# Attention and a low-rank mixer on one core: off-diagonal keys kept in place, later q and k turned by VectorE blocks and TensorE products, and another order of the work

## The chip, the cores and the metric

The kernel runs on one core of one Trainium2 chip. The core has TensorE (matrix products, with PE in the profile; its weight loads are PEld), VectorE (DVE), ScalarE (ACT), GpSimd (POOL) and SyncE (SP), and 16 DMA engines that move data between HBM and on-chip memory (SBUF). Products land in PSUM, which has eight banks. Each engine runs its own list of instructions in the order in which the program issued them, and waits on semaphores for the others. The metric is device time in microseconds (us), the median of three runs.

## The reference

Four sequences of 768 tokens with 8 heads of 64 go through attention with a sliding window and a few global keys, and the result through a mixer and a two-layer network:

```
scores = q @ k.T / 8 - slope[h] * dist        # dist: distance back, 96 for a global key outside the window
keep   = (key < 8) or (0 <= query - key < 96)
x      = softmax(scores where kept) @ v       # heads side by side: (4, 768, 512)
h      = (x.T @ U @ V).T                      # U: 768 x 32, V: 32 x 768
u      = x + h
out    = u + relu(u @ w1) @ w2                # w1: 512 x 2048, w2: 2048 x 512
```

Inputs and output are float32; the kernel computes in float16 with float32 sums.

## The kernel before, in words

The work is cut into 16 *pairs* (batch `b`, two heads), `p = 4b + hp`, each done by `attention(p)`, and four batches of `mlp(b)`. Tokens come in six blocks of 128.

**Loads (`add_load`, lines 439 to 496).** q, k and v of a pair are fetched from float32 HBM into float16 staging tiles by DMAs that GpSimd issues (`lk`, `lq`, `lv`; lines 453, 457, 461). Pairs 0 to 6 fetch rows of several tokens in one DMA; pairs 7 to 15 fetch q and k in two DMAs each, with 64 numbers of one token (256 B in HBM, 128 B in SBUF) as the piece. The weights come in eight DMAs (`w1_`, `w2_`; L503, L512), also from GpSimd.

**Turning (`EK`, `EQ`).** Scores need q and k with the 64 features on the partitions. Pairs 0 to 6 are turned by TensorE (`tr`, L600: twelve transposes of 128x64 each for q and for k, on half of the array's columns) and copied out of PSUM by ScalarE or VectorE. Pairs 7 to 15 are turned by DMA transposes issued from SyncE (L624).

**Off-diagonal keys.** A block of 128 queries looks at its own block of keys and at 96 keys of the block before together with 32 slots that hold the global keys. For k the 32 global columns are appended to every block (`KO`, one copy of 128x5x32), and the product reads columns 32 to 160. For v the 96 rows must move by 32 partitions (`vo`): GpSimd does it in three copies for pairs 0 and 1, and a DMA from SyncE (L651) for the others; a fourth copy on GpSimd brings the global rows (L368).

**Attention.** For batch 0 a bias product (`SB`, L689: identity times a table per head) comes ahead of the scores (`S`, L708); for later batches the exponential (`EX`, L735, ScalarE) is multiplied by a mask (`MK`, VectorE). `PV` (L804, L805) multiplies by v with a column of ones for the sums; `RC` and `NM` divide; `XC` casts x to float16; `UP` (L778, L788) turns x by products with the identity and multiplies it by U; `TE` copies x.T U out, `HM` (L911) multiplies by V, and `E` copies u, turned, to `uT`. For pairs 12 to 15 x is turned by a DMA transpose instead (`XD`, L880), and VectorE adds it in `E`.

**Network.** `M1a`/`M1b` (L967) are 512 products of 384 columns, `RL` (L984) the relu on ScalarE. The second layer multiplies 2x2 blocks with seven products (`P1` to `P7`, L1047) instead of eight, with sums on VectorE before (`PA`, `PB`) and after (`DA` to `DH`, L1060); `O` stores rows from SyncE.

**Order.** Nothing is issued as it is written. `add` collects tasks with an engine, an assumed duration, what they need and which buffers they take. `Planner.run` plays them through, and where several tasks of an engine are ready it takes the one with the lowest number in the table `PRIO`; the resulting start times sort the program. In the first part, where the plan leaves TensorE without work, products of zeros (`idle`, L1118) are put in.

Of the kernel before, what the change touches and what calls it, by code (L numbers as in the profile page):

```python
# [16 lines left out]
PE, ACT, DVE, POOL, SP = "PE", "ACT", "DVE", "POOL", "SP"  # L17


PRIO = {  # L20
    "DA0.1": 9974.7, "DA1.1": 2084.0, "DA1.2": 1446.2, "DA2.1": 7573.6, "DA2.2": 168.5, "DB0.0": 381.3,
    "DB0.1": 824.4, "DB0.2": 1435.8, "DB1.0": 648.9, "DB1.1": 9380.8, "DB1.2": -715.0, "DB2.0": 1750.3,
    "DB2.1": 7394.5, "DB2.2": 921.0, "DB3.0": 4247.8, "DB3.1": 1752.8, "DC0.0": 1445.9, "DC0.1": 241.1,
    "DC0.2": 3950.9, "DC1.2": -1125.0, "DC3.0": 4597.3, "DD0.0": -369.8, "DD0.1": 1451.6, "DD0.2": 7547.4,
    "DD1.0": 5644.0, "DD1.2": 1790.9, "DD2.2": 1857.9, "DD3.0": 9079.6, "DE0.0": 4526.5, "DE0.1": 4818.3,
    "DE0.2": 1899.6, "DE1.0": 1079.9, "DE1.1": 1235.7, "DE1.2": 9688.2, "DE2.0": 9329.5, "DE2.1": 7182.2,
    "DE3.1": 408.9, "DF0.0": -587.1, "DF0.1": 906.3, "DF0.2": 1308.3, "DF1.0": 1987.4, "DF1.1": 4335.1,
    "DF1.2": 9220.2, "DF2.1": 1119.2, "DG0.0": 1566.3, "DG0.1": 1561.2, "DG0.2": 4753.1, "DG1.1": 1049.2,
    "DG2.0": 1258.8, "DG3.0": 8393.9, "DH0.1": -943.2, "DH0.2": 7144.0, "DH1.0": 4329.3, "DH1.2": 1416.7,
    "DH2.0": 1090.1, "DH2.2": 9290.0, "E01": 680.8, "E012": 6952.3, "E015": 6662.8, "E02": 1709.4,  # L30
    "E03": 7455.6, "E115": 6744.6, "EK1": 1092.1, "EK11": 1175.1, "EK2": -4286.2, "EK3": 1889.8,
    "EQ0": 5977.3, "EQ1": 1795.7, "EQ2": 3871.2, "EQ3": 1123.3, "EQ4": 2337.6, "EQ5": -70.1,
    "EX0.0": 136.1, "EX0.1": 619.4, "EX0.2": 1542.8, "EX1.0": -44.8, "EX1.2": 651.6, "EX10.0": -3388.7,
    "EX10.1": -4484.6, "EX11.0": 671.9, "EX12.0": 259.7, "EX12.1": 848.5, "EX13.1": 2805.7, "EX14.0": -4053.9,
    "EX15.0": 325.5, "EX15.1": 1245.1, "EX2.2": 459.5, "EX3.2": -4609.0, "EX4.0": 2040.9, "EX4.1": 708.4,
    "EX5.1": -3545.6, "EX5.2": 2671.0, "EX6.0": 277.4, "EX7.1": 1490.6, "EX8.0": 484.1, "EX8.1": 473.6,
    "EX9.0": -4173.8, "EX9.1": 528.5, "HM1": 7237.6, "HM10": 1056.5, "HM11": 2789.4, "HM12": 193.4,
    "HM13": 4578.0, "HM14": 2924.3, "HM4": 1390.4, "HM6": 6847.2, "HM7": 7112.0, "HM8": 875.8,
    "KO1": 4413.7, "KO10": 4820.4, "KO13": 1045.3, "KO4": 1558.1, "KO6": 7458.7, "KO8": 810.0,
    "KO9": 5696.5, "MK10.1": -64.6, "MK10.2": 8941.2, "MK11.0": 1790.4, "MK11.1": 6926.2, "MK11.2": 4176.4,  # L40
    "MK12.1": 9457.0, "MK12.2": 9396.4, "MK14.0": 1575.4, "MK15.0": 2089.4, "MK5.0": 1157.0, "MK5.1": 4456.1,
    "MK5.2": 4026.8, "MK6.1": 1969.0, "MK6.2": 8473.4, "MK7.0": 1965.2, "MK7.2": 8877.9, "MK8.0": 4742.7,
    "MK8.2": 7363.9, "NH3.0": 1052.5, "NH3.1": 4293.2, "NH3.2": -718.0, "NM0": 3502.3, "NM10": -3.6,
    "NM12": 745.7, "NM13": 4324.7, "NM2": 956.8, "NM3": 8933.0, "NM4": 6531.1, "NM6": 9302.7,
    "NM8": 8671.5, "NM9": 5709.1, "P10.0": 8038.9, "P10.1": 3749.7, "P10.2": 1100.2, "P11.0": 7486.8,
    "P11.1": 779.5, "P11.2": 890.3, "P12.0": 258.9, "P12.1": 1917.5, "P12.2": -195.3, "P13.0": 1231.1,
    "P13.1": 5474.6, "P13.2": 1092.0, "P20.0": 6169.2, "P20.1": 6444.0, "P20.2": 1493.3, "P21.0": 81.1,
    "P21.1": 196.4, "P21.2": 6738.9, "P22.0": 7741.1, "P22.1": 7201.7, "P22.2": 4091.2, "P23.0": -41.9,
    "P23.1": 1721.9, "P23.2": 7210.2, "P30.0": 7173.3, "P30.1": 6570.0, "P30.2": 1800.3, "P31.0": 7984.8,
    "P31.1": 4608.1, "P31.2": 1074.6, "P32.0": 284.8, "P32.1": 7089.9, "P32.2": 738.2, "P33.0": 8514.1,  # L50
    "P33.2": 9035.8, "P40.0": 8007.7, "P40.1": 3973.5, "P40.2": 6133.8, "P41.0": 3854.4, "P41.1": 7361.7,
    "P41.2": 6492.4, "P42.1": 7111.9, "P42.2": 1850.0, "P43.0": 5388.4, "P43.1": -217.2, "P43.2": 8297.9,
    "P50.0": 7151.2, "P50.1": 7171.5, "P50.2": 1808.9, "P51.0": 6511.1, "P51.1": 3837.9, "P51.2": 806.0,
    "P52.0": 2789.2, "P52.1": 7444.2, "P52.2": 988.2, "P53.0": 3222.2, "P53.1": 8488.0, "P53.2": 5964.3,
    "P60.0": 1544.3, "P60.1": 7428.3, "P60.2": 6759.4, "P61.0": 3319.6, "P61.1": 3970.3, "P61.2": 5190.3,
    "P62.0": 6224.9, "P62.1": 7152.4, "P62.2": 804.9, "P63.0": 4221.3, "P63.1": 480.6, "P63.2": 802.1,
    "P70.0": 6565.8, "P70.1": 8670.9, "P70.2": 4740.0, "P71.0": 6930.4, "P71.1": 3484.2, "P71.2": 2866.8,
    "P72.0": 5944.4, "P72.1": 7444.2, "P72.2": 7101.8, "P73.0": 5747.6, "P73.1": 6207.0, "P73.2": 4226.5,
    "PA0.1": 3875.7, "PA1.1": 4773.6, "PA2.3": 4018.7, "PB0.0": 4368.4, "PB0.1": 3979.1, "PB1.0": 4691.2,
    "PB1.1": 4947.3, "PB1.2": 581.7, "PB1.3": 5664.9, "PB2.1": 9613.8, "PB2.2": 6977.8, "PB2.3": 1205.4,  # L60
    "PV1": 953.8, "PV10": 6764.8, "PV11": 1576.6, "PV12": 7016.6, "PV13": 4620.5, "PV14": 4609.9,
    "PV2": 4453.8, "PV3.1": 7591.7, "PV3.2": 6559.2, "PV4": 3559.8, "PV5": 5520.0, "PV6": 6732.0,
    "PV8": 8381.2, "PV9": 6620.1, "RC1": 1068.7, "RC10": -348.8, "RC3.0": 85.5, "RC3.1": 1705.7,
    "RC3.2": 1515.9, "RC4": 1577.1, "RC5": 572.7, "RC6": 9411.2, "RC9": 4947.8, "RS0.0": 623.7,
    "RS0.1": 7972.9, "RS0.2": -1247.9, "RS1.0": 667.2, "RS1.1": 4419.1, "RS1.2": 657.7, "RS2.0": 6902.5,
    "RS2.1": 3723.0, "RS2.2": 7418.7, "RS3.0": 200.0, "RS3.1": -174.3, "RS3.2": 8.1, "S0.0": 1224.9,
    "S0.1": 1257.7, "S0.2": 597.8, "S1.1": 6958.1, "S1.2": 408.5, "S10.2": 925.1, "S11.0": 2116.4,
    "S11.2": 2864.1, "S12.0": 7724.4, "S12.2": 1228.1, "S13.0": 2772.6, "S13.2": 6865.5, "S14.0": 1199.9,
    "S14.2": 2407.7, "S15.0": 1398.4, "S15.2": 4794.4, "S2.0": 7510.6, "S2.2": 4999.8, "S3.0": 1728.1,
    "S3.2": 3575.4, "S4.0": 7303.6, "S4.2": 7813.1, "S5.0": 7633.1, "S5.2": 6453.5, "S6.0": 1492.8,  # L70
    "S6.2": 2826.3, "S7.0": 2695.5, "S7.2": 5594.9, "S8.0": 6717.1, "S8.2": 6990.7, "S9.0": 3459.0,
    "S9.2": 6262.8, "SB0.0": 1291.1, "SB0.1": 514.3, "SB0.2": 7692.8, "SB1.0": 430.4, "SB1.1": 599.9,
    "SB1.2": 4615.8, "SB2.0": 7063.3, "SB2.1": 4782.3, "SB2.2": 7308.6, "SB3.0": 531.8, "SB3.1": 6967.6,
    "SB3.2": 6911.1, "TD0": 7030.0, "TE0": 3966.3, "TE1": 675.6, "TE10": 4461.6, "TE11": 280.5,
    "TE12": 4818.6, "TE13": 4022.1, "TE14": 1818.3, "TE2": 4322.3, "TE3": 1059.7, "TE5": 4885.8,
    "TE6": -68.9, "TE7": 251.6, "TE8": 9276.7, "TE9": 4286.1, "TK4": 7905.3, "TK5": 5413.1,
    "TK6": 4414.1, "TQ1": 2668.8, "TQ2": 7693.4, "TQ3": 6828.5, "TQ5": 1864.3, "TQ6": 4764.5,
    "TWa0": 9550.6, "UP0": 7074.6, "UP1": 7827.2, "UP10": 2854.9, "UP11": 953.4, "UP12": 6809.4,
    "UP13": 7067.4, "UP14": 1956.0, "UP15": 791.9, "UP2": 6544.2, "UP3.0": 7443.0, "UP4": 3868.9,
    "UP5": -1290.3, "UP6": 7978.5, "UP7": 8833.1, "UP8": 5191.3, "UP9": 2150.7, "VO1.0": 7116.1,  # L80
    "VO1.2": -3290.1, "VO10": 1203.0, "XC0": 7540.7, "XC1": 1666.3, "XC10": 7434.6, "XC15": 2000.5,
    "XC2": -2725.2, "XC4": 6510.6, "XC5": 7203.3, "XC6": 7832.2, "XC7": -638.1, "back": 5810.4,
    "bias0": 1175.4, "bias1": 986.6, "bias2": 2210.6, "bias3": 7209.7, "bias4": 8335.5, "bias5": 1191.5,
    "bias6": 6089.3, "bias7": 7006.4, "lk1": -135.8, "lk11": 6090.1, "lk15": 7280.7, "lk2": 972.8,
    "lk3": 6441.1, "lk4": 7540.3, "lk5": 7421.1, "lk6": 7505.4, "lq1": 927.0, "lq13": 4852.5,
    "lq2": 6424.7, "lq3": 6999.5, "lq4": -3610.8, "lq5": 7812.9, "lv0": 5693.9, "lv1": 7056.6,
    "lv15": 7968.8, "lv2": -2525.5, "lv3": 8233.4, "lv4": 6565.3, "lv5": 9127.7, "lv8": 7499.0,
    "mask0": 2297.1, "mask1": 589.7, "mask2": 775.8, "mask3": 1722.4, "mask4": 1692.7, "mask5": 2036.9,
# [176 lines left out]
def kernel(  # L265
# [13 lines left out]
    nc = tc.nc  # L279
# [888 lines left out]
```

## Time and profile before

| what | value |
|---|---|
| median of 3 runs | 234.32 us (233.78 to 234.71) |
| profiled execution, first to last instruction (its span) | 231.3 us |
| median less span | 3.0 us |
| granted TensorE clock | 1.000 |
| TensorE busy | 223.4 us, 97% |
| VectorE busy | 153.1 us, 66% |
| ScalarE busy | 118.7 us, 51% |
| GpSimd busy | 90.2 us, 39% |

The span is the profiled execution's own time on the engines; no separate total of that execution is given, so the 3.0 us between it and the median of the other runs is taken as what lies around the span. TensorE is the engine to follow: it has almost no idle time after the first 30 us. A matmul's busy time in the profile includes its way through the array, so products that follow each other overlap in it; the rate is read from the distance between starts. A "first part" below means the time until the first `M1a`, at 35.1 us.

### The profile page before, as it was taken

The page shows a single profiled execution, that of the slowest core. Times are in us where ns is not written, and L with a number is a line of the kernel's source. Part 1 is how long each engine was busy: PE and PEld are TensorE (multiplying, and loading weights), DVE is VectorE, ACT ScalarE, POOL GpSimd, SP SyncE. Part 2 cuts the span into 40 slices and gives each one's busy share as a digit, 9 for nine tenths or more (in the row PEclk, how much of TensorE's full clock was granted, in tenths as well). Part 3 has the DMA queues.
Part 4 walks back from the last instruction along what each step waited for, and adds up shares of the span by engine and source line. Part 5 has one row for each costly group of instructions (what it writes and reads, how often), then busy time and mean ns, then how long its engine had stood idle before and what let it go on. Part 6 is the DMA issues. An engine that isn't in the chain of part 4 may idle for free.

```text
span 231.3 us, 5732 instructions
## 1 busy us (share of the span) xinstructions
PE 223.4 (97%) x2402; PEld 158.3 (68%) x2402; DVE 153.1 (66%) x321; ACT 118.7 (51%) x161; POOL 90.2 (39%) x116
## 2 busy tenths in 40 slices
PE   7889999999999999999999999999999999999993
PEld 2556675565788885656678885666689875658882
DVE  6548772499987975375867785395888840626762
ACT  3576978878632446766652228868610025662000
POOL 9789968349929960264800911030100000000000
PEclk9999999999999999999999999999999999999999
DMA  7999999999999999992961995221020630000025
GB/s 169 162 163 150 156 189 211 207 188 166 167 157 160 175 166 235 219 123 22 130 56 41 162 162 173 56 41 30 15 22 17 157 136 4 0 0 3 0 84 191
DMA packets 89642, 26.96 MB, mean 117 GB/s; under 512 B 77040, under 2 KB 86640, under 8 KB 89616
## 3 DMA queue, kind: packets, MB, share of 16 engines
q0 software_dynamic: 63616, 13.24, 69.3%
q1 hardware_dynamic: 26000, 13.35, 27.3%
q8 instruction: 19, 0.31, 0.5%
q14 instruction: 7, 0.06, 0.1%
HBM read 27.46 MB, written 6.29 MB: 146 GB/s over the span
## 4 chain that ended last, share of the span: by engine, by line
PE 84%; POOL 7%; DMA 6%; issue 1%; ACT 0%; DVE 0%; POOLq 0%
PE ps L967 37%; PE ps L1047 33%; PE ps L708 4%; DMA vt<-in_v_dram 3%; DMA stgk<-in_k_dram 3%; PE ps L805 2%; PE ps L788 2%; POOL vo L368 2%; PE ps L804 2%; PE ps L1035 1%; POOL stgk L453 1%; POOL vt L461 1%; PE ps L778 1%; PE ps L911 1%; POOL stgq L453 1%
## 5 line engine op out<-in xcount | busy, mean ns | idle before, releaser
L967 PE MATMUL ps<-uT,w 128*128 128x384 f16 x512 | 88.1, 326 | 0.3 <-ACT uT L364 0.3
L967 PEld LDWEIGHTS <-w 128*128 128x128 f16 x512 | 48.1, 98 | 32.2 <-issue 1.0
L984 ACT ACTIVATE htr<-ps 128x768 f16<-128x768 f32 x64 | 51.9, 811 | 32.4 <-PE ps L967 32.2
L735 ACT ACTIVATE ep<-ps 128x1024 f16<-128x1024 f32 (+1 forms) x48 | 44.1, 952 | 16.0 <-PE ps L708 15.9
L1047 PEld LDWEIGHTS <-htr 128*128 128x128 f16 x384 | 36.1, 98 | 6.5 <-issue 2.0
L1047 PEld LDWEIGHTS <-sA 128*128 128x128 f16 x288 | 27.5, 98 | 3.8 <-issue 0.5
L461 POOL DMA_DIRECT2D vt<-in_v_dram x16 | 16.5, 1031 | 34.4 <-PE ps L805 27.9
L748 DVE TENSOR_TENSOR ep<-ep,mask 128x1024 f16<-128x1024 f16 x24 | 16.6, 691 | 16.4 <-ACT ep L735 16.4
L1060 DVE TENSOR_TENSOR x_sb<-ps,x_sb 128x256 f32<-128x256 f32 x48 | 19.9, 421 | 9.9 <-PE ps L1047 9.4
L1047 PE MATMUL ps<-w,htr 128*128 128x256 f16 x192 | 24.5, 273 | 0.0
L1047 PE MATMUL ps<-tB,htr 128*128 128x256 f16 x192 | 24.4, 273 | 0.0
L1047 PE MATMUL ps<-w,sA 128*128 128x256 f16 x192 | 24.4, 273 | 0.0
L368 POOL COPY vo<-vt 32x650 f16<-32x650 f16 x22 | 18.1, 823 | 9.5 <-DMA vt<-in_v_dram 8.9
L1001 DVE TENSOR_TENSOR sA<-htr 128x768 f16<-128x768 f16 x16 | 9.5, 594 | 18.3 <-ACT htr L984 18.1
L364 ACT ACTIVATE u<-ps 128x256 f32<-128x256 f32 x12 | 4.6, 384 | 29.7 <-PE ps L1047 29.7
L869 POOL CAST x<-x_sb 128x768 f16<-128x768 f32 x12 | 10.8, 906 | 22.7 <-DVE x_sb L843 12.8
L457 POOL DMA_DIRECT2D stgk<-in_k_dram x18 | 14.8, 834 | 3.8 <-PE ps L967 3.8
L708 PEld LDWEIGHTS <-kT 64*128 64x128 f16 x352 | 10.1, 94 | 8.9 <-issue 8.1
L457 POOL DMA_DIRECT2D stgq<-in_q_dram x18 | 14.9, 838 | 3.1 <-DMA w<-in_moe_w_ch_dram 3.1
L708 PE MATMUL ps<-qT,kT 64*128 64x128 f16 x352 | 15.6, 218 | 0.0
L843 DVE TENSOR_TENSOR x_sb<-ps,rcp 128x768 f32<-128x768 f32 x16 | 15.2, 956 | 0.4
L1060 DVE TENSOR_TENSOR u<-ps,u 128x256 f32<-128x256 f32 x24 | 10.0, 419 | 6.7 <-PE ps L1047 4.9
(78 smaller groups left out, 272.2 us busy)
## 6 DMA issues: line engine op xcount, KB each, us to landing
out_dram<-x_sb SPq DMA_DIRECT2D x23, 256.0 KB, 2.6
w<-in_moe_w_ch_dram POOLq DMA_DIRECT2D x8, 512.0 KB, 9.2
vt<-in_v_dram POOLq DMA_DIRECT2D x16, 192.0 KB, 7.1
stgk<-in_k_dram POOLq DMA_DIRECT2D x18, 96.0 KB, 6.8
stgq<-in_q_dram POOLq DMA_DIRECT2D x18, 96.0 KB, 6.2
vo<-vt SPq DMA_DIRECT2D x14, 121.9 KB, 4.9
stgk<-in_k_dram POOLq DMA_DIRECT2D x6, 192.0 KB, 6.7
stgq<-in_q_dram POOLq DMA_DIRECT2D x6, 192.0 KB, 6.6
```

The costliest lines, as they stand in the source:

```text
L368: nc.gpsimd.tensor_copy(dst, src)
L457: nc.gpsimd.dma_start(o[:, :, hi], src[b, h0 + hi].rearrange("(n p) d -> p n d", p=P))
L461: nc.gpsimd.dma_start(vt[gv.slot][:, :, :, 0:D], v[b, h0:h0 + 2].rearrange("h (n p) d -> p h n d", p=P),)
L708: nc.tensor.matmul(t[:, hi, j * P:(j + 1) * P], lhs, qt[r, i * P:(i + 1) * P], start=not biased, stop=True, skip_group_check=biased,)
L735: nc.scalar.activation(ep[gep.slot][:, :, lo:512], ps[:, gsc.slot:gsc.slot + 2, lo:512], AF.Exp, scale=qk_scale)
L748: nc.vector.tensor_tensor(ev, ev, mv, ALU.mult)
L843: nc.vector.tensor_tensor(xo, pvo()[:, :, :, 0:D], rcp[p % 2].unsqueeze(3).broadcast_to((P, 2, NB, D)), ALU.mult)
L869: (nc.vector if xe == DVE else nc.gpsimd).tensor_copy(x16[gx16.slot], src)
L967: nc.tensor.matmul(ps[:, g.slot + half, 0:HS], w1[:, dc, jt * P:(jt + 1) * P], ub[:, dc, half * HS:(half + 1) * HS], start=(dc == 0), stop ...
L984: nc.scalar.activation(htr[:, jt].rearrange("p (h c) -> p h c", h=2), ps[:, g.slot:g.slot + 2, 0:HS], AF.Relu)
L1047: nc.tensor.matmul(o, a[:, j, c0 + cols.start:c0 + cols.stop], bq[:, j], start=False, stop=(j == hj - 1), skip_group_check=True,)
L1060: return lambda: e.tensor_tensor(o(), x(), y(), ALU.add)
```

## The change

Five things change together.

1. *Keys in place.* Block i's 96 earlier keys stay on the slots where they are, and the global keys take slots 0 to 31. So k's neighbours are copied to a tile of their own, `kO` (two copies, 128x5x96 and 128x5x32), and `vo` becomes a copy on the same partitions (128x660, then 32x660 for the globals). Both are given to VectorE, ScalarE or GpSimd pair by pair (`KO`, `VO` in `CFG`); only pair 15's `vo` is a DMA.
2. *Turning of pairs 4 to 15.* There is no DMA transpose left. Pairs 5, 7, 9, 11, 13, 15 are turned by one VectorE transpose of 32x32 blocks for q and one for k, from a load in which each partition holds 24 pieces of 32 numbers (128 B in HBM, 64 B in SBUF). Pairs 4, 6, 8, 10, 12, 14 are turned by six 128x128 TensorE transposes and one copy by ScalarE or VectorE.
3. *x and U.* x of pairs 12 to 15 is turned by TensorE like the others. For nine pairs (`NU`) the product with U has x as the fixed operand and 32 columns moving, and one more product (`XU`) turns the result after a copy (`XE`).
4. *Bias.* Eight scaled identities (128x128) replace the eight bias tables (128x384).
5. *Order.* `PRIO` and the choice in `Planner.run` are gone; a list of all tasks, `ORDER`, is walked in its order. Engines of many small copies (`TE`, `XE`, `XC`, `E`, casts of pair 0) are set pair by pair.

The parts of the diff that the prediction speaks of:

```diff
+    "TK": "PPPPPDPDPDPDPDPD", "TQ": "PPPPPDPDPDPDPDPD", "NU": (4,5,6,8,9,10,12,13,14), "back": "KO1", "TE": "ADAAAAAAADDADAAA", "XE": "DDDDDAADAADDDADD", "EK": "ADDDDAAAAAAAAAAA", "EQ": "DADAAAAAAAAAAAAA", "KO": "ADDDDPAPPPADDAPP",
+    "VO": "DDPDDPDPPPPPAPDS", "XC": "DDPDPAAPDPPAPPPP", "E": "AADAAAAAADAAAADA",
...
+                    o = dst[g.slot].rearrange("p a b -> p (a b)")
+                    for i in range(2):
+                        nc.gpsimd.dma_start(
+                            o[64 * i:64 * i + 64], src[b, h0 + i].rearrange("(t k) (j e) -> j t k e", t=TB, j=2)
+                        )
...
-        def dtr(dst, gd, stg, gs):
-            def go():
-                o = dst[gd.slot]
-                nc.sync.dma_start(
-                    o[:, :, 0:P] if dst is kT else o.rearrange("c (n p) -> c n p", n=NB),
-                    stg[gs.slot].rearrange("p a b -> p (a b)"), transpose=True,
-                )
...
+        def turn(dst, stg, gs):
+            def go():
+                nc.vector.transpose(
+                    dst().rearrange("c (t k) -> c k t", t=TB),
+                    stg[gs.slot].rearrange("p a b -> p (a b)").rearrange("p (k e) -> p k e", e=TB),
+                )
...
+        def flip(g, stg, gs):
+            def go():
+                for n in range(NB):
+                    nc.tensor.matmul(
+                        ps16[:, g.slot, n * P:(n + 1) * P],
+                        stg[gs.slot].rearrange("p a b -> p (a b)")[:, n * P:(n + 1) * P],
+                        ident16, is_transpose=True, start=(n == 0), stop=(n == NB - 1),
+                    )
...
         def koff():
-            kt = kT[gkT.slot]
-            copy(ke, kt[:, 0:NB - 1, P:PK], kt[:, 0:1, 0:32].broadcast_to((P, NB - 1, 32)))
+            kt, ko = kT[gkT.slot], kO[gkT.slot]
+            copy(ke, ko[:, :, GP:P], kt[:, 0:NB - 1, GP:P])
+            copy(ke, ko[:, :, 0:GP], kt[:, 0:1, 0:GP].broadcast_to((P, NB - 1, GP)))
...
-    order = pl.run()
+    c_back.deps.append(pl.names[CFG["back"]])
+    order = pl.run(ORDER)
```

Counted in the two programs: DMA transposes 22 and 0; `vo` DMAs 14 and 3; TensorE products of zeros 74 (8 of 512 columns, 66 of 128) and 28 (7 and 21). The end of `ORDER` is `P33.1 DG3.2 O3.5 DF3.1 P33.2 DH3.1 O3.1 DH3.2 O3.2`: the last store is now a half row block (128 KB), where the last one before is a full one (256 KB).

## The prediction, on record before the changed kernel ran

> **What bounds the kernel now.** I read the page's first two parts, then what TensorE waits for, then TensorE's timeline of the first part, then the DMA stretches and issues.
>
> ```profile
> span 231.3 us, 5732 instructions
> PE 223.4 (97%) x2402; PEld 158.3 (68%) x2402; DVE 153.1 (66%) x321; ACT 118.7 (51%) x161; POOL 90.2 (39%) x116
> ...
> PE   7889999999999999999999999999999999999993
> ...
> DMA  7999999999999999992961995221020630000025
> ```
>
> TensorE works without a gap from slice 4 to the end. So an edit counts by the TensorE products that it adds or removes, by a wait of TensorE that it ends or starts, or by the tail. The DMA digits show transfers crowded until about 105 us and sparse after.
>
> ```profile
> PE ps L600 <- DMA stgk<-in_k_dram: 1.7, 2, 1.1
> PE ps L1118 <- POOL zero L379: 1.3, 1, 1.3
> PE ps L778 <- ACT uT L364: 0.4, 1, 0.4
> PE ps L967 <- ACT uT L364: 0.3, 1, 0.3
> ```
>
> These are all of TensorE's open waits (total, number, longest). Of 231.3 - 223.4 = 7.9 us without work, 1.3 are before the first product and 3.8 after the last, which leaves 2.8. But other waits are filled with products of zeros:
>
> ```profile
> 4.96 0.85 PE L600 MATMUL ps<-ident,stgk 128*64 128x128 f16 x12
> 7.22 0.55 PE L600 MATMUL ps<-ident,stgk 128*64 128x128 f16 x12
> ...
> 28.83 0.49 PE L778 MATMUL ps<-ident,x 128*128 128x128 f16 x6 [0.38 <-ACT uT L364]
> 29.16 0.50 PE L788 MATMUL ps<-x,u 128*128 128x128 f16 x6
> 29.50 0.49 PE L911 MATMUL ps<-vs,tmp 128*128 128x384 f16 x2
> 29.92 0.53 PE L600 MATMUL ps<-ident,stgk 128*64 128x128 f16 x12
> 30.38 0.51 PE L778 MATMUL ps<-ident,x 128*128 128x128 f16 x6
> ...
> 32.28 0.94 PE L1118 MATMUL ps<-zero 128*128 128x128 f16 x14
> 33.29 0.53 PE L600 MATMUL ps<-ident,stgk 128*64 128x128 f16 x12
> 33.75 0.62 PE L1118 MATMUL ps<-zero 128*128 128x128 f16 x8
> ```
>
> Columns: start, busy time, engine, line, operation, count. Rates are read between starts: six 128-column products take 0.33 us (28.83 to 29.16), so 56 ns each. At 32.28 TensorE has nothing but zeros until the k of pair 5 lands at 33.29: 22 zero products stand around that wait. They are no work, and cost 56 ns each (the eight wide ones at the start 0.42 each, 2.96 us from 1.32 to 4.28 for seven starts).
>
> **The change part by part.** The sum is made against the profiled execution's 231.3 us; the median of the runs is 3.0 us above it, taken as constant.
>
> *TensorE work.* (a) Turning: a change of array tiling costs 0.08: the same two `HM` products take 0.42 with a half-width turn behind them (29.50 to 29.92) and 0.34 with full-width products (31.94 to 32.28). A half-width turn (twelve) takes 0.46 (29.92 to 30.38) less 0.08. Before 14 x 0.38 = 5.3; after 8 x 0.38 + 12 x 0.33 = 7.0: +1.7. I price the plain 128x128 turns as other 128-column products. (b) x and U: six products 0.33. Before 12 x 0.67 + 4 x 0.33 = 9.4. After 16 x 0.33 for x, 7 x 0.33 for U, and nine times six 32-column products and one of 128. A 32-column product isn't in the trace: between 14 ns (the array's time by columns, from 56 for 128) and 29 ns (the products of 65 columns in L804 and L805 start 30 ns apart, each with fresh weights). I take 29, the nearer row in kind: 5.3 + 2.3 + 9 x 0.23 = 9.7, so +0.3 (-0.5 at 14 ns). The Trainium skill, "TensorE: Matmul & The Clock Gate", Part 1, gives 25 ns for 32 columns; by that this term would be 0.2 us less. No run here shows it. (c) `HM`: full height 0.34, half height 0.16 (61.67 to 61.83); two more pairs are at half height: -0.35. (d) Changes of array tiling between neighbouring tasks, counted along the two orders: 107 and 90; -17 x 0.08 = -1.4. Sum of a to d: +0.25, from -0.55 to +0.25.
>
> *Zero products.* 8 wide and 66 narrow become 7 and 21: -0.42 - 45 x 0.056 = -2.95. They leave only if the waits that they fill leave. What ends them: GpSimd no longer makes ten copies of `vo` (0.82 each) in the first part, which stood between its DMA issues; after, two `vo` copies and two small `vs` copies stay there. The loads of k 3, q 3, k 2 now go out ahead of the first v, in the order in which TensorE takes them; and pair 5, whose k was late at 33.29, is scored after the first network tiles.
>
> *Open waits.* Of 2.8 us I take 0.8 away: half of the 1.7 for k, and the 0.3 at 88 us, where a score task now stands between `E17` and the `M1b` that needs it, less 0.35 for new ones. Ends: -2.8 (all go) and +2.0 (as much again as two of the present k waits).
>
> *Tail.* Before, the last store is 256 KB, after 128 KB:
>
> ```profile
> out_dram<-x_sb SPq DMA_DIRECT2D x23, 256.0 KB, 2.6
> ...
> out_dram<-x_sb SPq DMA_DIRECT2D x2, 128.0 KB, 1.9
> ```
>
> (KB, us to landing.) That is up to -0.7; the full store issued just ahead is still on its way, so I take -0.4 (0 to -0.7).
>
> *VectorE.* Added: 12 block transposes, not in the trace, between 0.55 (mask product of 768 columns) and 0.96 (copy of 768 from PSUM; nearest, one element at a time): 11 us; 12 `vo` copies of 660 at about 0.4 (384 columns of scaling take 0.25 unhindered): 5; 12 `kO` copies 3.6, PSUM copies of turned q and k 1.9, `XE` 1. Removed: 16 `KO` 5.1, twelve of 16 `TE` 3.4, the sums with xT 2.4, `vs` and a cast of q 3.2, bias 1.8. Net +7 on 153, or 70% of the span. Cover: the 78 us in which VectorE is idle. In the densest stage, 165 to 185, it is busy 17.45 of 20; there `TE` and `E` move to ScalarE (busy 3.4) and a cast of 0.78 to GpSimd. Nothing on the path at 0.96; if a transpose took 1.5, the mask products and divisions queued behind it would be late in turn.
>
> *ScalarE, GpSimd, SyncE.* ScalarE gains some 15 us of small copies (118.7 to about 134): the exponentials of pairs 6, 10, 13 queue behind their `kO` copies, covered by its 112 idle us. GpSimd: `vo` 22 to 16 copies, -5; six `kO` pairs +6; three fewer casts -2.7; the second issue per load of pairs 4 to 6 and longer ones for 64-byte pieces (1.03 as for v with as many pieces, against 0.83), +8. A `kO` on GpSimd waits for the turned k, and with it the loads queued behind. SyncE loses 22 transposes and 11 copies; only stores remain. U and V are fetched after `KO1` (about 3 us later); 7.3 to landing still ends some 7 us before the first `UP`.
>
> *Transfers.* The new q and k loads of six pairs have 3072 pieces of 64 B per tensor, against 1536 of 128.
>
> ```profile
> 135.00:137.50 2.50, 2.50 (x25) 1.79 (x23) 2.00 (x7) 0.97 (x2) 0.00 (x0) 1.00 2.41 154
> 39.00:48.00 9.00, 9.00 (x78) 5.31 (x77) 4.69 (x8) 7.76 (x10) 2.81 (x5) 1.00 1.24 206
> ```
>
> The last number is GB/s. At 135 a backlog of 128-byte pieces drains: 154 GB/s / 128 B = 1200 per us, or 13.3 ns on each of 16 engines. At 39 it is weights in 1024-byte pieces: 79 ns each. The line through both gives 8.6 ns for 64 B; the upper end is a fixed price, 13.3. Per tensor that is 1.7 to 2.6 us; I take 2.6, the nearest piece. A pair so loaded takes 5.1 + 1.3 for v, the other kind 3.9, so two pairs 10.3 of about 26 us: covered. Nothing is added.
>
> *Sum.* +0.25 - 2.95 - 0.8 - 0.4 = -3.9: span 227.4, time 234.3 - 3.9 = **230.4**.
>
> **The rivals.** *Slower: the 64-byte pieces are late.* Place: pairs 5 and 7, whose loads share the crowded stretch until 105 us with the weights. Against: the line above, and idle transfers in 105 to 108.5, 118 to 126, 146 to 153. For: no row below 128 B but 4-byte flags. At twice 13.3 ns a pair takes 5.1 us more; two such pairs in the crowded stretch, +10.2: 240.6. It decides when they lose 3.9 + 1.2 us together, at 20 ns a piece. The Trainium skill, "DMA: Bandwidth & Descriptors", Specifications, says that pieces below 512 B fall under line rate because they are read, changed and written back; the 128-byte row, at 154 against 206 GB/s, agrees. Whether 64 B pays more per piece no run here shows. Chance 0.13.
>
> *No change: the waits stay.* The zeros go, but TensorE waits for ScalarE's exponentials instead: 234.3 + 0.25 - 0.4 = 234.2. For: ScalarE is busy 12.6 of 15 us from 15 to 30. Against: the wait that ends the first part is a load (33.29). Chance 0.11.
>
> *VectorE becomes the bound.* At 1.5 a transpose, 12 x 0.54 = 6.5 more, all of it on the path: 236.9. Chance 0.03.
>
> *The clock comes late.* Twelve turns take 0.85 at 4.96 and 0.55 at 7.22: TensorE is slow in its first 7 us, and there are fewer zeros to raise it. Were it slow for as long again (5.9 us, in which it works eight or nine tenths), half of that work time, 2.5 us, would be lost: 232.9, still faster. Against: only one of the eight wide zero products is missing at the start. Chance 0.04. The Trainium skill, "TensorE: Matmul & The Clock Gate", Part 1, has the clock rise only after about 3.4 us of steady work; that rule speaks against the change, and the trace agrees that the rise comes after some 6 us of zeros and turns.
>
> **How the numbers follow.** Likeliest, 0.69: 230.4, its own range 228.5 to 233.0 (open waits, tail and 32-column products at their ends, partly together). The range reaches up over "no change", 228.5 to 235.2, and leaves out the slower rivals and a few in 100 below. A measurement tells about 0.5% here, 233.15 to 235.5. Faster 0.73 (0.69 and the late clock's 0.04), same 0.11, slower 0.16 (0.13 and 0.03).
>
> **What would show it.** Right: some 28 zero products in 4.2 us, the first `M1a` near 31 us, no open wait on L600, block transposes of 0.8 to 0.96, 64-byte loads landing in 5 to 7 us after issue, DVE busy near 160. Wrong: waits of TensorE for VectorE or for stgk and stgq after 40 us; 32-column products above 30 ns; an L967 that starts later than 33 us.

## The result, and the profile after

The changed kernel takes 559.85 us (median of 4 runs, 558.47 to 562.1) against 234.05 (4 runs, 232.5 to 234.71): 2.395 times as long, with an interval of 2.384 to 2.407. The forecast of 230.4 us, and its whole range, was wrong. In the profiled execution the span is 558.5 us, against 231.3 before.

From the page of the changed kernel: the span, the busy times of the engines, the busy digits of TensorE and its granted clock in 40 slices, and the DMA packets by size; the last line is that of the kernel before.

```profile
span 558.5 us, 5687 instructions
PE 249.6 (45%) x2389; PEld 173.9 (31%) x2389; DVE 192.5 (34%) x321; ACT 136.3 (24%) x198; POOL 178.9 (32%) x129
PE   9504055940016624010000724607819131999997
PEclk9957557975558856555555855957968656899999
DMA packets 350425, 22.12 MB, mean 40 GB/s; under 512 B 340768, under 2 KB 347424, under 8 KB 350400
DMA packets 89642, 26.96 MB, mean 117 GB/s; under 512 B 77040, under 2 KB 86640, under 8 KB 89616
```

TensorE's row of nines has become islands with empty slices between them, and no engine is busy for half of the span: everything waits. The clock falls to five tenths in the empty stretches (0.716 on average) and is back at eight and nine tenths in the last 15% of the span, where TensorE works almost without a gap. The packets are the odd thing: fewer bytes than before (22.12 against 26.96 MB), yet 350,425 packets against 89,642.

Two groups of instructions that did not exist before (busy us, mean ns of one | idle time before them and what ended it):

```profile
L386 POOL DMA_DIRECT2D stgk<-in_k_dram x12 | 50.5, 4210 | 132.6 <-issue 122.0
L507 DVE STREAM_TRANSPOSE kT<-stgk 128x768 f16<-128x768 f16 x6 | 22.2, 3693 | 48.2 <-DMA stgk<-in_k_dram 47.7
```

L386 is the load of the pairs that VectorE turns. The instruction alone takes GpSimd 4.2 us where I had put 1.03, and ahead of ten of the twelve GpSimd stands for some 12 us on nothing that the profile shows ("issue"). The q loads on the same line are alike. The block transposes take 3.7 us where I had put 0.96.

Now who waits, from the list of waits (us in total, times, longest), and the timelines of GpSimd and, in the last line, of TensorE where it happens first:

```profile
PE ps L702 <- POOL vo L302: 122.8, 5, 48.4
PE ps L676 <- POOL x L765: 105.4, 3, 66.7
POOL stgk L386 <- issue: 122.0, 10, 15.9
```

```profile
20.73 4.23 POOL L386 DMA_DIRECT2D stgk<-in_k_dram  x1 [4.38 <-PE ps L703]
37.39 4.21 POOL L386 DMA_DIRECT2D stgk<-in_k_dram  x1 [12.43 <-issue]
41.59 0.81 POOL L420 DMA_DIRECT2D w<-in_moe_w_ch_dram  x1
42.38 1.55 POOL L302 COPY vo<-vt 128x660 f16<-128x660 f16 x2
...
54.44 4.22 POOL L386 DMA_DIRECT2D stgq<-in_q_dram  x1 [9.39 <-issue]
71.51 4.20 POOL L386 DMA_DIRECT2D stgq<-in_q_dram  x1 [12.85 <-issue]
...
43.98 0.21 PE L702 MATMUL ps<-vo,ep 128*128 128x65 f16 x1 [21.24 <-POOL vo L302]
```

The first DMA of pair 5's k goes out at 20.73. The second one stands behind it in GpSimd's list and comes only at 37.39; behind that stand a load of weights and two `vo` copies, which end at 43.93. TensorE, which needs those copies for `PV`, stands still for 21.24 us until 43.98. The next two, of q, are 17.07 us apart. With the casts of x to float16 and the copies `kO` (39.7 us), which stand in the same list, TensorE's waits for GpSimd add up to 268 of the 309 us in which it does nothing. Over the whole span the 24 issues take 24 x 4.21 = 101.0 us and the waits ahead of them 122.0 + 120.2 = 242.2 (k and q): together 343 us, against the 327.2 us by which the span grew. The packets in the trace also say how long GpSimd stands: until about 1 us after the last packet of the DMA before (36.58 and then 37.39; 70.58 and 71.51; 126.07 and 127.07). So the trace points at GpSimd's list, which stands while these transfers run. It does not say what in the load costs so much, nor what the slow transposes would do by themselves.

### The profile page after: what moved, and what is told of

It is laid out like the page before. It is cut to its first block, busy times and chain, and to the rows that moved or that the text cites. A ratio compares the mean times of both kernels' runs of the same rounds, so it can differ in the third digit from the quotient of the medians.

```text
span 558.5 us, 5687 instructions
## 1 busy us (share of the span) xinstructions
PE 249.6 (45%) x2389; PEld 173.9 (31%) x2389; DVE 192.5 (34%) x321; ACT 136.3 (24%) x198; POOL 178.9 (32%) x129
## 2 busy tenths in 40 slices
DMA packets 350425, 22.12 MB, mean 40 GB/s; under 512 B 340768, under 2 KB 347424, under 8 KB 350400
## 4 chain that ended last, share of the span: by engine, by line
issue 47%; PE 23%; POOL 18%; DMA 9%; DVE 1%; POOLq 0%; DVEq 0%
PE ps L840 10%; PE ps L919 7%; POOL stgk L386 6%; POOL stgq L386 6%; DMA stgq<-in_q_dram 4%; DMA stgk<-in_k_dram 3%; DMA vt<-in_v_dram 2%; POOL vo L302 2%; POOL vt L392 1%; POOL stgk L382 1%; PE ps L608 1%; POOL stgq L382 1%; PE ps L989 1%; PE ps L676 1%; DVE kT L507 1%
## 5 line engine op out<-in xcount | busy, mean ns | idle before, releaser
L840 PE MATMUL ps<-uT,w 128*128 128x384 f16 x512 | 95.9, 349 | 0.0
L386 POOL DMA_DIRECT2D stgk<-in_k_dram x12 | 50.5, 4210 | 132.6 <-issue 122.0
L386 POOL DMA_DIRECT2D stgq<-in_q_dram x12 | 50.5, 4208 | 120.2 <-issue 120.2
L702 PE MATMUL ps<-vo,ep 128*128 128x65 f16 x160 | 15.0, 213 | 122.8 <-POOL vo L302 122.8
L676 PE MATMUL ps<-ident,x 128*128 128x128 f16 x96 | 11.6, 250 | 105.4 <-POOL x L765 105.4
L703 PEld LDWEIGHTS <-ep 128*128 128x128 f16 x192 | 15.8, 110 | 125.5 <-issue 123.8
L676 PEld LDWEIGHTS <-x 128*128 128x128 f16 x96 | 8.7, 113 | 107.6 <-POOL x L765 106.7
L507 DVE STREAM_TRANSPOSE kT<-stgk 128x768 f16<-128x768 f16 x6 | 22.2, 3693 | 48.2 <-DMA stgk<-in_k_dram 47.7
L608 PE MATMUL ps<-qT,kO 64*128 64x128 f16 x160 | 15.3, 249 | 45.2 <-POOL kO L302 39.7
L507 DVE STREAM_TRANSPOSE qT<-stgq 128x768 f16<-128x768 f16 x6 | 22.2, 3696 | 12.2 <-DMA stgq<-in_q_dram 8.7
```

Source lines behind the costliest of these rows:

```text
L386: nc.gpsimd.dma_start(o[64 * i:64 * i + 64], src[b, h0 + i].rearrange("(t k) (j e) -> j t k e", t=TB, j=2))
L507: nc.vector.transpose(dst().rearrange("c (t k) -> c k t", t=TB), stg[gs.slot].rearrange("p a b -> p (a b)").rearrange("p (k e) -> p k e", ...
L608: nc.tensor.matmul(t[:, hi, j * P:(j + 1) * P], lhs, qt[r, i * P:(i + 1) * P], start=not biased, stop=True, skip_group_check=biased,)
L676: nc.tensor.matmul(ps[:, gx.slot + c // 3, (c % 3) * P:(c % 3 + 1) * P], xx[:, c], ident16, start=(c % 3 == 0), stop=False, skip_group_che ...
L702: nc.tensor.matmul(o, e[:, hi, j * P:(j + 1) * P], vof[:, hi, i - 1, 0:D1], start=True, stop=False)
L703: nc.tensor.matmul(o, e[:, hi, (j + 1) * P:(j + 2) * P], vv[:, hi, i, 0:D1], start=(i == 0), stop=True)
```

## The experiments

**The disputed operations by themselves.** My first theories on the load: the 64-byte piece is dear by its size ("size"); something goes by the number of partitions of a DMA ("partitions"); or it is the shape of this access, (half, 32 groups of tokens, 24 tokens, 32 numbers) ("shape"). For the transposes: they are slow in any form, or because each result stands 24 columns (48 bytes) from the one before. The kernel holds only such loads, one at a time (`took` is a small VectorE copy that waits for the load, and the next load waits for it), and VectorE operations; ahead of them stand stores of zeros, so that the output is written:

```diff
+        # the load of the changed kernel: 64 partitions (j t), 24 pieces of 32 numbers
+        g.dma_start(s_a[0:64].rearrange("p (k e) -> p k e", e=32), k0.rearrange("(t k) (j e) -> j t k e", t=32, j=2))
+        took(s_a)
+        # half of it: 32 partitions (t), 24 pieces of 32 numbers
+        g.dma_start(s_a[0:32].rearrange("p (k e) -> p k e", e=32), k0.rearrange("(t k) (j e) -> j t k e", t=32, j=2)[0])
...
+        # the transpose of the changed kernel: results 24 apart
+        nc.vector.transpose(d_a.rearrange("c (t k) -> c k t", t=32), s_b.rearrange("p (k e) -> p k e", e=32))
...
+        # results side by side
+        nc.vector.transpose(d_a.rearrange("c (k t) -> c k t", t=32), s_b.rearrange("p (k e) -> p k e", e=32))
```

> A kernel that computes nothing of the reference: nine loads, one after the other, and eight VectorE instructions, each alone. The reference load is 128 partitions x 6 pieces of 64 numbers; the load of the changed kernel is 64 partitions x 24 pieces of 32. Theory 'size': every load with pieces of 64 B in SBUF brings some 7 transfers of 4 B for each piece (so 128 x 6 pieces of 32 numbers too: over 5000 of them, 5 us or more), loads with 128-byte pieces none. Theory 'partitions': the extra transfers come with destinations of fewer than 128 partitions, whatever the piece; the 128 x 6 x 32 load is clean and lands in under 3 us. Theory 'shape': only the load with (j t) in front, four counted dimensions, has them. Block transposes: 3.7 us as in the changed kernel with results 24 columns apart; if the distance of the results sets that, under 1.0 us with results side by side, and if the transpose itself is slow, 3.7 in all forms.

Its timeline, GpSimd first (the changed load and its half), then VectorE (transpose as in the change; with results side by side; with operands 24 apart and results side by side; a plain copy with results 24 apart and side by side):

```profile
16.93 4.22 POOL L68 DMA_DIRECT2D s_a<-in_k_dram  x1 [11.18 <-DVE one L62]
34.20 0.71 POOL L71 DMA_DIRECT2D s_a<-in_k_dram  x1 [13.04 <-DVE one L62]
```

```profile
55.73 3.69 DVE L93 STREAM_TRANSPOSE d_a<-s_b 128x768 f16<-128x768 f16 x1
63.19 0.98 DVE L96 STREAM_TRANSPOSE d_a<-s_b 128x768 f16<-128x768 f16 x1
65.21 1.50 DVE L99 STREAM_TRANSPOSE d_a<-s_b 128x768 f16<-128x768 f16 x1
66.75 1.93 DVE L101 COPY d_a<-s_c 128x768 f16<-128x768 f16 x1
68.72 0.36 DVE L103 COPY d_a<-s_c 128x768 f16<-128x768 f16 x1
```

The changed load takes 4.22 us of GpSimd and 16.8 us until its data is there. (The last packet of the stores ends at 22.6, before most of this load's; on an idle chip a load of the same kind, in the second attempt below, takes as long, 17 us.) The same 64-byte pieces fetched one half at a time take 0.71 us and land 2.6 us after the issue, and loads with 32, 64 and 128 partitions are all quick. 768 pieces of 128 bytes land no sooner, 2.9 us after their issue. "Size" and "partitions" fall; it is the shape. The trace's packets say in what: the quick loads move their pieces and 16 packets of 4 bytes, the changed one 10,752 packets of 4 bytes, seven to each of its 1536 pieces. (On the queue of GpSimd's DMAs the changed kernel has 259,296 of 4 bytes, the one before 1,152; 24 x 10,752 is 258,048 of them.)

The transposes are slow by the distance of their results: 3.69 against 0.98 side by side, and a plain copy pays too, 1.93 against 0.36. The Trainium skill, "Advanced Engine Details and Errata", Memory Cachelines, says that SBUF has lines of 16 bytes and that an access which goes to another line each time is slower; with results 48 bytes apart every write does so, and these rows agree, though no run here varies the distance, so the line as the reason is not shown.

**Which feature of the shape, first attempt.** The loop over the halves is the outermost of the access, and in HBM its step (128 bytes) is smaller than those inside it: the halves are interleaved. Theory "interleaved": that is what costs. Rivals: two loops over partitions as such, or small pieces in so many partitions.

```diff
+        # neighbouring tokens as halves: pieces of 64 numbers
+        g.dma_start(s_a[0:64].rearrange("p (k e) -> p k e", e=64), k0.rearrange("(t k w) e -> w t k e", t=32, w=2))
+        took(s_a)
+        # two heads as halves: pieces of 32 numbers
+        g.dma_start(s_a[0:64].rearrange("p (k e) -> p k e", e=32), kh.rearrange("h (t k) (j e) -> j h t k e", t=32, j=2)[0])
...
+        # the changed load again, pieces of 16 numbers in four quarters
+        g.dma_start(s_a[:, 0:384].rearrange("p (k e) -> p k e", e=16), k0.rearrange("(t k) (j e) -> j t k e", t=32, j=4))
```

> Computes nothing of the reference: six loads, one after the other, each alone, to find what in the load of the changed kernel (64 partitions, two interleaved halves of every token's 64 numbers) brings the 10752 transfers of 4 B. In order: that load again (4.2 us on GpSimd, about 11 us of transfers); two halves that interleave, but with pieces of 64 numbers; two halves that do not interleave (two heads), pieces of 32; interleaved halves on 32 partitions; two heads, pieces of 64; four interleaved quarters with pieces of 16 on 128 partitions. Theory 'interleaved': every load whose outer step in HBM is smaller than its inner one is bad, the second, fourth and sixth too. Theory 'small and interleaved': the fourth and sixth are bad, the second clean. Theory 'small and two groups of partitions': the third is bad too. Where none fits, only the first and the sixth are.

GpSimd's timeline, these three in their order:

```profile
34.52 2.60 POOL L69 DMA_DIRECT2D s_a<-in_k_dram  x1 [25.38 <-DVE one L62]
44.84 0.96 POOL L72 DMA_DIRECT2D s_a<-in_k_dram  x1 [7.72 <-DVE one L62]
...
62.27 4.25 POOL L81 DMA_DIRECT2D s_a<-in_k_dram  x1 [2.91 <-DVE one L62]
```

Every interleaved load was slow and the load of two heads quick, so "interleaved" seemed to hold. But the packets of 4 bytes say more than slow and quick: with two halves there are 5,376 for 768 pieces, seven to a piece as before, and with four quarters 9,216 for 3072 pieces, three to a piece. 7 is 16/2 - 1 and 3 is 16/4 - 1. And the load of two heads was no fair rival: head and token steps fit together there, so its two loops are one of 64.

**Which feature, second attempt.** New theory "short loop": with n the length of the outermost loop, after joining loops that fit, each piece brings 16/n - 1 packets of 4 bytes, interleaved or not. Heads 0 and 2 make a loop of 2 that is neither interleaved nor joinable; and interleaved tokens can be fetched with a loop of 16, 8 or 4 outside:

```diff
+        ka = k[0, 0:4].rearrange("(a b) s d -> b a s d", b=2)[0]
...
+        g.dma_start(s_a[0:64].rearrange("p (k e) -> p k e", e=32), ka.rearrange("h (t k) (j e) -> j h t k e", t=32, j=2)[0])
...
+        g.dma_start(s_a[:, 0:384].rearrange("p (k e) -> p k e", e=64), k0.rearrange("(t k w) e -> w t k e", t=8, w=16))
...
+        g.dma_start(s_a[:, 0:384].rearrange("p (k e) -> p k e", e=64), k0.rearrange("(t k w) e -> w t k e", t=16, w=8))
...
+        g.dma_start(s_a[:, 0:384].rearrange("p (k e) -> p k e", e=64), k0.rearrange("(t k w) e -> w t k e", t=32, w=4))
```

> Five loads of k alone, one after another (it computes nothing of the reference). The extra packets of 4 bytes were 7 to a piece with two interleaved halves, and counted again in the run before, 3 to a piece with four interleaved quarters (9,216 for 3072 pieces), and the pair of heads there was no fair rival: its two loops over partitions join into one of 64. 7 = 16/2 - 1 and 3 = 16/4 - 1, so a new theory, 'short loop': what counts is the length n of the outermost loop that can't be joined with the next, and a piece gets 16/n - 1 extra packets, interleaved or not. Theory 'interleaved' as before. The loads and what each expects: (1) the changed load, both 10,752 extra packets and 4.2 to 4.3 us on GpSimd. (2) heads 0 and 2, a loop of 2 that is not interleaved and can't be joined, 1536 pieces: 'short loop' 10,752 and 4.2 us, 'interleaved' none beyond 16 and 0.7 to 1.0 us. (3) interleaved tokens with a loop of 16 outside, 768 pieces: 'short loop' 16 and under 1 us, 'interleaved' thousands and over 2 us. (4) the same with a loop of 8: 'short loop' 768, (5) with a loop of 4: 'short loop' 2304 and between 1 and 2 us; 'interleaved' 5,376 and over 2 us for both, as for two halves of 768 pieces.

```profile
34.58 4.21 POOL L69 DMA_DIRECT2D s_a<-in_k_dram  x1 [25.43 <-DVE one L62]
52.12 0.82 POOL L72 DMA_DIRECT2D s_a<-in_k_dram  x1 [13.33 <-DVE one L62]
55.41 1.18 POOL L75 DMA_DIRECT2D s_a<-in_k_dram  x1 [2.47 <-DVE one L62]
60.08 1.83 POOL L78 DMA_DIRECT2D s_a<-in_k_dram  x1 [3.49 <-DVE one L62]
```

In the order of the diff the packets of 4 bytes beyond the 16 of each load are 10,752, none, 768 and 2,304 (counted by size in the trace): 7, 0, 1 and 3 to a piece. "Interleaved" falls at the first two lines and "short loop" holds in all four. The Trainium skill, "DMA: Bandwidth & Descriptors", Why a DMA increments its semaphore by 16 and not by 1, says that a DMA is spread over the largest number of engines up to 16 that divides the lengths of the slowest dimensions; a loop of 2 gives two engines. The counts fit that, as if each remaining group of engines were given an empty transfer for every real one. So do the data pieces: for 768 pieces of 128 bytes the sum of their own times, over the time from the first one's start to the last one's end, is 4.2, 7.1, 13.5 and 28.1 for n of 2, 4, 8 and 16, so the number under way at one time about doubles with n. Which engines carry them no run here shows, nor how much of the delay is due to the empty packets and how much to the few pieces under way.

GpSimd's own time follows all the packets that a load brings, pieces and empty ones together: 4.21 us for 12,288 (1536 pieces, n = 2) and 4.25 for as many again (3072 pieces, n = 4), 2.60 and 2.36 for 6,144, 1.83 for 3,072, 1.18 for 1,536 and 0.82 for 768. The quick load of 1536 pieces, without empty ones, took 0.96.

**One fault at a time in the whole kernel.** First the changed loads with a plain copy in place of the transposes:

```diff
-                nc.vector.transpose(
-                    dst().rearrange("c (t k) -> c k t", t=TB),
-                    stg[gs.slot].rearrange("p a b -> p (a b)").rearrange("p (k e) -> p k e", e=TB),
-                )
+                nc.vector.tensor_copy(dst(), stg[gs.slot].rearrange("p a b -> p (a b)"))
```

> The loads of the changed kernel with 64-byte pieces stay, each VectorE block transpose is replaced by a copy of the same 768 columns (so q and k of pairs 5, 7, 9, 11, 13, 15 are not turned and the scores of these pairs are not the reference's). Theory 'loads': 500 us or more, GpSimd's load instructions still 4.2 us, with waits of some 12 us ahead of them. Theory 'transposes': under 300 us, since 12 x 3.7 us of VectorE are gone.

Measured: 555.83 us (one run), with the loads' group as before: 4.21 us each, 119.7 us of waits ahead of those of k. With VectorE relieved of 36 us (156.2 busy against 192.5) the kernel stays where it was, 4 us below. The loads alone make practically the whole loss.

Then the transposes with the loads of the other pairs:

```diff
-                elif how == "P":
+                else:
                     o = dst[g.slot].rearrange("p a b -> p (a b)").rearrange("p (n h d) -> p h n d", n=NB, h=2)
                     for i in range(2):
                         nc.gpsimd.dma_start(o[:, i], src[b, h0 + i].rearrange("(n p) d -> p n d", p=P))
-                else:
...
```

> The block transposes stay, the loads of pairs 5, 7, 9, 11, 13, 15 are the ones of 128-byte pieces that the other later pairs use (so the transposes work on another layout and the scores of these pairs are not the reference's). Theory 'loads': under 270 us: 12 x 2.8 us more VectorE work than planned, at most 33 us over some 231, and no transfers of 4 B beyond the flags. Theory 'transposes': over 400 us.

Measured: 260.87 us (one run; the kernel before on that chip 233.13). The transposes take 3.7 us as in the change. The longest of TensorE's waits:

```profile
PE ps L602 <- DVE qT L501: 10.8, 3, 4.1
PE ps L602 <- POOL kO L302: 7.3, 2, 4.8
```

The loads are quick now, and still TensorE waits for the turned q and for `kO`, which is copied from the turned k. They take 12 x (3.70 - 0.97) = 33 us more of VectorE than side by side, and the kernel is about 29 us longer than the version below. VectorE is busy only 73% of the span, but on the chain of work that ended last, on the page of this run, the transposes have 13% of the span, some 33 us. This run differs from that version in its loads too.

**Both faults mended.** One half of one head at a time, so the loop of 32 groups of tokens is the outermost (four DMAs per tensor, on 32 partitions each); tokens taken in the order (k t), so that the transposes write side by side. The list of tasks is that of the change; only the durations that the planner assumes for these loads and transposes are set to the new forms.

```diff
-                    for i in range(2):
+                    for i in range(4):
                         nc.gpsimd.dma_start(
-                            o[64 * i:64 * i + 64], src[b, h0 + i].rearrange("(t k) (j e) -> j t k e", t=TB, j=2)
+                            o[32 * i:32 * i + 32].rearrange("t (k e) -> t k e", e=TB),
+                            src[b, h0 + i // 2].rearrange("(k t) (j e) -> j t k e", t=TB, j=2)[i % 2],
                         )
...
-                    dst().rearrange("c (t k) -> c k t", t=TB),
+                    dst().rearrange("c (k t) -> c k t", t=TB),
```

> Both faults mended, the rest as in the changed kernel and its order: each half of each head comes in a DMA of its own (32 partitions, 24 pieces of 32 numbers, tokens of a partition 32 apart), and the block transpose then writes its results side by side. Theory 'these two forms are all that is wrong': 12 transposes of 1.0 us, no extra transfers, GpSimd's loads 2.9 us per tensor instead of 8.4; the time comes down to what was forecast, 229 to 234. If four DMAs per tensor hold up the loads of the later pairs, TensorE waits for them after 40 us and it ends at 234 to 240. Theory 'more is wrong': over 240.

Measured: 231.98 us (7 runs, 230.43 to 232.51) against 233.65 (10 runs): ratio 0.9915, interval 0.9878 to 0.9952. So the rest of the change, with these two forms mended, is a small gain. The page, the group of the k transposes, and TensorE's longest open waits:

```profile
span 230.2 us, 5720 instructions
PE 220.0 (96%) x2389; PEld 158.5 (69%) x2389; DVE 164.2 (71%) x321; ACT 135.0 (59%) x198; POOL 112.0 (49%) x153
...
L508 DVE STREAM_TRANSPOSE kT<-stgk 128x768 f16<-128x768 f16 x6 | 5.8, 970 | 0.1
```

```profile
PE ps L677 <- POOL x L766: 1.7, 2, 1.1
PE ps L703 <- POOL vo L302: 1.5, 1, 1.5
```

The clock is 1.000 again. The transposes take 0.97, as I had priced them, and the 48 load issues take GpSimd 0.73 each, 35 us in place of 343 with their waits.

**No block transposes at all.** All of pairs 4 to 15 are turned by plain TensorE products; the twelve new tasks and their copies are put into the order near the places of the old ones (the start of the changed `CFG` line, and the order as shown for pair 7).

```diff
-    "TK": "PPPPPDPDPDPDPDPD", "TQ": "PPPPPDPDPDPDPDPD",
+    "TK": "PPPPPPPPPPPPPPPP", "TQ": "PPPPPPPPPPPPPPPP",
...
-HM4 E04 lv6 P10.0 TQ6 EQ6 TWb1 PB0.0 DI0.0 PB0.2 P50.0 lk8 TK6 PV5 EK6 P50.1 KO6 lk10 mask7 P60.1 mask6 RC5 DI0.1
+TQ6 EQ6 TWb1 PB0.0 DI0.0 PB0.2 P50.0 lk8 TK6 PV5 TK7 EK6 TQ7 P50.1 KO6 EQ7 EK7 lk10 mask7 P60.1 mask6 RC5 DI0.1 S6.2
```

> All twelve later pairs are turned by plain TensorE products from 128-byte pieces; keys in place, x and U, bias and the order of the list stay, with twelve turns put in and their copies moved next to them. TensorE gets 12 x 0.33 = 4.0 us more work than the changed kernel was to have. Theory 'loads or transposes alone': 230.4 + 4.0 = 234.4, between 231 and 237, no wait of TensorE over 2 us after the first part. Theory 'the rest of the change costs too' (copies of kO and vo, the order): 240 or more, with waits of TensorE for kO, vo or x.

Measured: 232.46 us (10 runs, 231.47 to 233.16) against 233.13 (13 runs): ratio 0.9946, interval 0.9911 to 0.998. The theory "loads or transposes alone" holds; the rest of the change does not lose time. Span 230.9, TensorE busy 224.3, VectorE 149.7. Twelve turns more on TensorE, 15 us less on VectorE, and 0.7 us more of span than the mended blocks: turning by VectorE, done well, is worth little here. No run compares the two side by side, and their intervals overlap. Both versions are faster than the kernel before by under 1%, but by more than their intervals.

## Why the prediction was wrong

*Transfers*, "Nothing is added", is the step that failed. I priced a 64-byte piece by its size alone, at 8.6 to 13.3 ns. The size is harmless, as the quick loads of 64-byte pieces show. What the rows before could not price is the order of the loops: every load of q, k and v in the old kernel has its 128 partitions as the outermost loop. By those prices a DMA of 1536 pieces moves in 0.8 to 1.3 us. With the halves outermost it took 17.07 us from issue to issue; 1536 pieces of the same size from two neighbouring heads were there 3.5 us after the issue.

*GpSimd's issue*, taken as 1.03 "as for v with as many pieces", was 4.21: again the number of pieces was the wrong measure. I counted eight microseconds more on GpSimd and let them cost nothing. That its list goes in order I said only of `kO`, which holds the loads behind it; I did not ask it of a load. A DMA that cannot go out holds the `vo` copies, the casts of x, the weights and the next loads behind it, and TensorE with them. Nor could the 1.03 have told of the wait, which lies outside the instruction (4.2 us) and is three times as long.

*The rival "the 64-byte pieces are late"* (chance 0.13) had the place right, the loads of pair 5 and of the others of its kind. Its mechanism was wrong, and its size: twice the price and 240.6 us. It put the harm on two pairs in the crowded stretch; ten of twelve k issues and ten of twelve q issues had to wait. The rule of the Trainium skill that stood beside it ("DMA: Bandwidth & Descriptors", Specifications), that pieces below 512 B fall under line rate, applies to the quick 64-byte loads as well; with 768 pieces landed 2.6 us after the issue, these runs do not bear it out as the cause.

*VectorE* failed too, hidden behind the first. The range of 0.55 to 0.96 came from rows whose results stand side by side, and side by side 0.97 is right. The change writes them 48 bytes apart, which the diff says (`"c (t k) -> c k t"`) and I did not read: 3.7. The rival "VectorE becomes the bound" was the right mechanism for that with too small a price. It put 1 us of time on each us of VectorE; in the one run with slow transposes and quick loads it is about 29 for 33.

*The clock comes late* was no cause. The clock of 0.716 follows the waits: it is five tenths in the empty slices, eight or nine in the full ones, and 1.000 when the loads are mended in the same order. In that mended kernel twelve turns take 0.68 at 6.07 us, so TensorE's slow start is no longer than before.

The rest of the sum can be read in the mended kernel, whose span is 1.1 us below that of before where I had 3.9. *Zero products*: 28, as counted. *Tail*: the last product starts at 226.44 against 227.16 and the span ends 3.7 after it against 4.1, about -0.35 for the -0.4. *TensorE work*: the 32-column products alternate with 128-column ones every 80 ns, so at 56 for the latter they take about 24 and not 29; with that, TensorE's busy time fell by 3.4 us (223.4 to 220.0) where the sum had 2.7. The first `M1a` starts at 31.73 (forecast near 31; before 35.1). The term with the wrong sign is *open waits*: I took 0.8 us away, and leaving out the start they rose from 2.4 to 5.4, of which 4.1 are for copies of `vo` and x by GpSimd and VectorE. That is +3.0 instead of -0.8, a difference of 3.8, and more than the 2.8 us by which the span misses the sum. Without the two faults the change takes 231.98 us, inside the range that I gave to the likeliest case, 228.5 to 233.0. It looks nearer to the forecast, 1.6 us off, than it is, and that is luck: the 3.0 us that I took for what lies around the span is 1.7 to 1.9 in the runs of the kernel before that list both, because the profiled execution was quicker than the median of the others. Too large a constant hid about 1.2 of the 2.8 us by which the span was missed.

## What to carry to other kernels

Price a transfer by the loops of its access and not by its piece alone: keep the partitions outermost, or another long loop (16, 32, 64 and 128 brought no empty packets here), split a DMA whose outermost loop is 2 or 4 into one per value, and watch the packet count on the page. Price a VectorE operation by where its results land: the order of the tokens was free here, and decided between 0.98 and 3.7 us. For an instruction that could be slow in an in-order list, ask first who stands behind it; here 24 loads alone made 233 us into 556.

## What was not expected of the hardware

- A load from GpSimd with an outermost loop of n brings 16/n - 1 packets of 4 bytes for each piece: 7, 3, 1 and 0 for n of 2, 4, 8 and 16. With 1536 pieces and n = 2 it takes 4.2 us of GpSimd and lands some 17 us after the issue, against 0.7 and 2.6 for its half, and 0.96 and 3.5 for as many pieces with n = 64.
- GpSimd then stands for some 12 us before its next such DMA (37.39 after 24.96). The trace names no releaser; it goes on about 1 us after the last packet of the DMA before (36.58).
- A block transpose of 768 columns takes 0.98 us with results side by side, 1.50 with operands 48 bytes apart, 3.7 with results 48 bytes apart; a copy 0.36 and 1.93.
